# Out product by seven products of quarters, with its sums on GpSimd, in a fused top-k attention and SwiGLU kernel

## The chip, the cores and the metric

The kernel runs on one core of one Trainium2 chip. The metric is the device time of one execution in microseconds (us). The profile names the engines PE (TensorE, matmuls), PEld (its weight loads), DVE (VectorE), ACT (ScalarE), POOL (GpSimd) and SP (SyncE, which issues the transfers). Each engine works through its own instructions in the order in which they were written, and engines wait for each other through semaphores.

## The reference

Attention keeps, in each row of scores, only the 32 largest; the result is laid out as 4608 tokens by 512 and goes through a gated feed-forward layer. All is fp32.

```python
# q, k, v: (8, 8, 576, 64); w_gate, w_val: (512, 1536); w_out: (1536, 512)
scores = scale * np.matmul(q, k.transpose(0, 1, 3, 2))
kth = np.partition(scores, -top_k, axis=-1)[..., -top_k:-top_k + 1]     # top_k = 32
scores = np.where(scores >= kth, scores, -1000000000.0)
attn = np.exp(scores - np.max(scores, axis=-1, keepdims=True))
attn = attn / (np.sum(attn, axis=-1, keepdims=True) + 1e-09)
x = np.matmul(attn, v).transpose(0, 2, 1, 3).reshape(B * S, H * D)
g = x @ w_gate
return g * (1.0 / (1.0 + np.exp(-g))) * (x @ w_val) @ w_out
```

## The kernel before

**Attention** goes in 160 units `n`: for each of 8 batches, four full tiles of 128 queries and a rest of 64, each for four pairs of heads. A unit with a rest has half the work. The loop over `n` (L524) holds, in program order: `normalize` of unit n-2 begins (POOL, L312), `penalize` of n-1 (POOL adds the scores to the mask, 128x1152, L293), `turn` of n-3 (PE transposes the weights, L329, ACT copies them out, L330), `values` of n-4 (PE, L349 and L358, ACT copies to `xT`, L373), `scores` of n+1 (PE, L250), `weigh` of n-1 (ACT exp, L302), the copies of the scores of n+1 (ACT, L255), and then the selection for unit n on DVE (L271, L275, L281). Between the steps of the selection stand the slots for the feed-forward layer, the end of `normalize` (DVE L314, ACT L317), and now and then the preparation of keys and queries (`fetch`, PE L205 and L197).

In this text **A** is the PE part of attention in one unit: transposes, values and scores, one after the other.

**The feed-forward layer** goes in 18 blocks `kb` of 256 tokens. `feed(kb)` is a generator. For each of six pairs of 128 columns of d_ff it makes a gate product and a value product (`product`, L412: 2 x 4 matmuls of 256 columns each, into one PSUM bank of `ps_f`, which has three). ACT takes each product out (L430 to L432, L437) and POOL multiplies (L433, L438), so that `h` stands as 128 columns of d_ff by 256 tokens, which is the form in which PE loads it as weights. The out product (L449) then makes, for each of two groups of 128 tokens, 12 matmuls of 512 columns that add up in one bank, with `h` as weights and `wo` as the moving operand. ACT copies the bank (L460) and SP stores it (L389). The block's `xT` buffer isn't read after the value products.

**Who sets the order.** `pieces(n)` draws up to n pieces from `feed` in slots of 2, 1, 1 and 6 per unit (L564, L572, L575, L578), as long as `credit` is at least 1. A piece is one half of a product or four matmul instructions' worth of the out product (two matmuls); each costs one credit. A full unit gets 4.6, a half unit 2.3, and at most 8 are saved up. A block can only begin when all its tokens have left attention (`done`, L479). What ACT and POOL have to do for a piece is put into `on_act` and `on_pool` and written out by `flush`: at the top of a unit (L545, L549), after the first slot (L565), or when more than one thing is waiting. At the end (L585 to L598) the order of each engine is fixed as it was written.

**Weights** come as 64-bit numbers and are rounded to fp32 in the kernel by `weights` (72 pieces, spread over the first units by `rounding`), with ACT, POOL and DVE at work on each.

Of the kernel before, what the change touches and what calls it, by code (L numbers as in the profile page):

```python
# [9 lines left out]
ALU = mybir.AluOpType  # L10
# [5 lines left out]
P = 128  # L16
# [4 lines left out]
BLK = 256  # L21
# [6 lines left out]
def kernel(  # L28
# [24 lines left out]

    nc = tc.nc
    B, H, S, D = q.shape
    DM, DFF = w_gate.shape
# [4 lines left out]
    KC = DM // P  # L63
    MC = DFF // P
    MS = MC // 2
    NBLK = B * S // BLK
    scale = 1.0 / float(D) ** 0.5
    assert D == 64 and R == 64 and H * D == DM and DM == 512 and B * S % BLK == 0
# [52 lines left out]
    def weights():  # L121
# [11 lines left out]
        for n in range(len(pieces) + lags[0]):  # L133
# [3 lines left out]
            ready[0] = max(n - lags[0] + 1, 0)  # L137
            yield

    ready = [0]  # L140
    weight = weights()

    def rounding(n):
# [254 lines left out]
    def feed(kb):  # L398
# [7 lines left out]
        def product(w, s, then):  # L406
            ps = ps_f.tile([P, 2, BLK], FP32, tag="f", name="f")
            need(8 * s + (4 if w is wg else 8))
            for i in range(2):
                m = 2 * s + i  # L410
                for kc in range(KC):
                    nc.tensor.matmul(  # L412
                        ps[:, i, :],
                        w[:, kc, m * P : (m + 1) * P],
                        x[:, kc, :],
                        start=(kc == 0),
                        stop=(kc == KC - 1),
                    )
                if i == 1:
                    on_act.append(lambda: then(ps))  # L420
                yield

        for s in range(MS):
            h = ffn.tile([P, 2, BLK], FP32, tag="h", name="h", bufs=MS + 1)
# [7 lines left out]
                nc.scalar.add(h[:], h[:], 1.0)  # L432
                on_pool.append(lambda: nc.gpsimd.tensor_mul(h[:], h[:], half[:]))  # L433

            def value(ps, h=h):
                val = ffn.tile([P, 2, BLK], FP32, tag="gv", name="val", bufs=3)
                nc.scalar.copy(val[:], ps[:])  # L437
                on_pool.append(lambda: nc.gpsimd.tensor_mul(h[:], h[:], val[:]))  # L438

            yield from product(wg, s, gate)  # L440
            yield from product(wv, s, value)
        for t in range(BLK // P):
            ps = ps_f.tile([P, DM], FP32, tag="f", name="o_ps")
            for m in range(MC):
                need(8 * MS + 2 * m + 2)
                if m == 6:
                    flush(on_act)
                    flush(on_pool)
                nc.tensor.matmul(  # L449
                    ps[:],  # L450
                    hs[m // 2][:, m % 2, t * P : (t + 1) * P],
                    wo[:, m, :],
                    start=(m == 0),
                    stop=(m == MC - 1),
                )
                if m == MC - 1:

                    def finish(ps=ps, t=t):
                        o = ffn.tile([P, DM], FP32, tag="o", name="o")
                        nc.scalar.copy(o[:], ps[:])  # L460
                        store(o, kb * BLK + t * P)

                    on_act.append(finish)
                if m % 2 == 1:
                    yield

    NU = len(units)
    todo = list(range(NBLK))
# [2 lines left out]
    def piece():  # L471

        if len(on_act) > 1:
            flush(on_act)
        if len(on_pool) > 1:
            flush(on_pool)
        while True:
            if not current:
                if not todo or done.get(todo[0], 0) < NHP * BLK:  # L479
                    return False  # L480
                flush(on_act)
                flush(on_pool)
                current.append(feed(todo.pop(0)))
            if next(current[0], 0) == 0:
                current.pop()
                continue
            return True

    def fetch(n):

# [6 lines left out]

    def pieces(n):
        for _ in range(n):
            if credit[0] >= 1 and piece():  # L500
                credit[0] -= 1

    def run(steps):
        for _ in steps:
# [19 lines left out]
    for n in range(NU + VALUES):  # L524
# [16 lines left out]
        if n >= NU - NHP:  # L541
            credit[0] = 8.0
        else:
            credit[0] = min(credit[0] + (4.6 if nh == 2 else 2.3), 8.0)
        flush(on_act)  # L545
        next(norm, None)
        if 0 <= n - 1 < NU:
# [81 lines left out]
```

## Time and profile before

| | us |
|---|---|
| median of 6 runs (lowest, highest) | 1914.99 (1913.37, 1916.08) |
| profiled execution, its own time | 1916.66 |
| its span from first to last instruction | 1914.9 |
| PE busy in the span | 1757.5 |
| DVE busy | 1609.0 |
| ACT busy | 1156.3 |
| POOL busy | 813.4 |

The span is the time from the first instruction to the last; the execution's own time has 1.8 us more around it. Busy times of PE are modelled, since matmuls overlap each other; a group's mean of one matmul is therefore longer than the distance from one to the next, and the pace of a run of matmuls is read from the starts in the timeline. One fp32 matmul of the program stands as two instructions in the profile. Before about 280 us the weights arrive and the pipeline fills; from there to about 1795 us the kernel is in a steady state; after 1847 us only the last block is left.

### The profile page before, as it was taken

What the parts mean: (1) busy time and instruction counts of PE and PEld (TensorE: products, weight loads), DVE (VectorE), ACT (ScalarE), POOL (GpSimd) and SP (SyncE); (2) the same over time, 40 slices, a digit from 0 to 9 for tenths busy, and PEclk for the clock granted to TensorE, in tenths of its full rate; (3) what the DMA queues carried; (4) which work ended last, traced back from release to release, by engine and by line L of the source; (5) the groups of instructions that cost most, each with busy time, mean ns of one, the idle gap of its engine ahead of it and who ended that gap; (6) DMA issues with size and microseconds to landing.
All of it is one profiled execution on the core that took longest, in us unless ns stands there. A gap on an engine that the chain in (4) does not pass through costs nothing.

```text
span 1914.9 us, 29363 instructions
## 1 busy us (share of the span) xinstructions
PE 1757.5 (92%) x10144; PEld 1298.7 (68%) x10144; DVE 1609.0 (84%) x3476; ACT 1156.3 (60%) x2821; POOL 813.4 (42%) x846
## 2 busy tenths in 40 slices
PE   3437789979999999999899999999999999999999
PEld 2326558667677777676768676868686868586866
DVE  7999889998899979998799979999799989999400
ACT  5656656566666656675657566656675656665421
POOL 4566644335343525353335343525243535253412
PEclk7577899989999999999999999999999999999999
DMA  7322202000300012000210003000210001000000
GB/s 184 88 78 83 67 22 68 11 1 2 72 17 12 2 27 62 12 1 13 53 37 1 12 3 87 1 12 1 58 32 12 1 14 45 18 1 12 1 12 11
DMA packets 111254, 59.58 MB, mean 31 GB/s; under 512 B 89089, under 2 KB 97281, under 8 KB 111105
## 3 DMA queue, kind: packets, MB, share of 16 engines
q1 hardware_dynamic: 109904, 57.41, 11.4%
q8 instruction: 80, 1.31, 0.3%
q14 instruction: 70, 0.57, 0.1%
q10 hardware_dynamic: 1200, 0.30, 0.1%
HBM read 48.23 MB, written 9.44 MB: 30 GB/s over the span
## 4 chain that ended last, share of the span: by engine, by line
PE 80%; DVE 7%; POOL 5%; ACT 4%; issue 3%; DMA 0%; SPq 0%; POOLq 0%; DVEq 0%; ACTq 0%
PE f L412 38%; PE o_ps L449 18%; PE av L358 7%; PE etps L329 7%; PE s L250 6%; DVE m L271 3%; DVE rest L275 3%; POOL e L293 2%; PE s L236 2%; PE av L349 1%; ACT e L302 1%; PE kqps L205 1%; ACT sc L255 1%; POOL size L113 1%; POOL size L103 1%
## 5 line engine op out<-in xcount | busy, mean ns | idle before, releaser
L271 DVE MAX8 m<-rest 128x8 f32<-128x576 f32 x864 | 615.3, 747 | 2.2
L275 DVE MATCH_REPLACE8 rest<-m,rest 128x576 f32<-128x576 f32 x576 | 424.2, 743 | 0.0
L412 PE MATMUL f<-xT,wg 128*128 128x256 f32 x1728 | 407.7, 386 | 0.0
L293 POOL TENSOR_TENSOR e<-e,sc 128x1152 f32<-128x1152 f32 (+1 forms) x160 | 382.5, 2390 | 43.6 <-DVE e L281 35.5
L412 PE MATMUL f<-xT,wv 128*128 128x256 f32 x1728 | 396.5, 381 | 0.0
L449 PE MATMUL o_ps<-wo,h 128*128 128x512 f32 x864 | 387.6, 598 | 0.0
L412 PEld LDWEIGHTS f<-xT,wg 128*128 128x128 f32 x1728 | 324.1, 191 | 71.5 <-issue 30.0
L412 PEld LDWEIGHTS f<-xT,wv 128*128 128x128 f32 x1728 | 326.0, 190 | 53.7 <-issue 10.6
L433 POOL TENSOR_TENSOR h<-h,half_g 128x512 f32<-128x512 f32 x108 | 138.2, 1279 | 453.7 <-ACT h L432 438.7
L271 DVE MAX8 m<-sc 128x8 f32<-128x576 f32 x288 | 205.7, 751 | 125.5 <-ACT sc L255 79.3
L329 PE MATMUL etps<-ident,e 128*128 128x128 f32 (+1 forms) x1312 | 188.2, 289 | 127.7 <-POOL size L103 46.9
L449 PEld LDWEIGHTS o_ps<-wo,h 128*128 128x128 f32 x864 | 159.4, 190 | 193.3 <-issue 186.5
L329 PEld LDWEIGHTS etps<-ident,e 128*128 128x128 f32 (+1 forms) x1312 | 160.2, 148 | 177.3 <-issue 54.2
L330 ACT COPY et<-etps 128x512 f32<-128x512 f32 (+1 forms) x448 | 184.7, 482 | 149.3 <-PE etps L329 148.0
L302 ACT ACTIVATE e<-e,bias 128x576 f32<-128x576 f32 x288 | 222.1, 776 | 76.6 <-POOL e L293 76.2
L317 ACT ACTIVATE e<-e,tot 128x576 f32<-128x576 f32 x288 | 210.4, 780 | 5.4 <-DVE tot L314 5.1
L275 DVE MATCH_REPLACE8 rest<-m,sc 128x576 f32<-128x576 f32 x288 | 211.9, 742 | 0.0
L438 POOL TENSOR_TENSOR h<-h,val 128x512 f32<-128x512 f32 x108 | 139.2, 1289 | 149.9 <-ACT val L437 149.9
L250 PE MATMUL s<-kqT 64*128 64x288 f32 x1024 | 173.9, 448 | 9.3 <-ACT kqT L210 5.7
L312 POOL TENSOR_SCALAR tot<-tot 128x2 f32<-128x2 f32 (+1 forms) x160 | 36.4, 227 | 330.7 <-ACT e L302 322.3
L358 PE MATMUL av<-et,v 128*64 128x128 f32 (+1 forms) x2560 | 172.6, 280 | 0.0
L255 ACT COPY sc<-s 128x288 f32<-128x288 f32 x512 | 165.1, 410 | 3.3 <-PE s L250 3.3
(44 smaller groups left out, 1436.1 us busy)
## 6 DMA issues: line engine op xcount, KB each, us to landing
kq_in<-in_k_dram SPq DMA_DIRECT2D x64, 128.0 KB, 2.9
v<-in_v_dram SPq DMA_DIRECT2D x32, 256.0 KB, 3.0
kq_in<-in_q_dram SPq DMA_DIRECT2D x62, 128.0 KB, 3.1
w<-in_moe_w_gate_dram SPq DMA_DIRECT2D x24, 256.0 KB, 2.8
w<-in_moe_w_val_dram SPq DMA_DIRECT2D x24, 256.0 KB, 2.7
w<-in_moe_w_out_dram SPq DMA_DIRECT2D x24, 256.0 KB, 2.6
out_dram<-o SPq DMA_DIRECT2D x40, 128.0 KB, 2.4
out_dram<-o SPq DMA_DIRECT2D x16, 256.0 KB, 2.3
```

What stands on the lines that cost most here:

```text
L250: nc.tensor.matmul(ps[:, 0:half], slab[d, q0 : q0 + P], slab[d, k0 : k0 + half])
L255: nc.scalar.copy(sc[:, i * half : (i + 1) * half], ps[:, 0:half])
L271: nc.vector.max(m[:, t, 8 * r : 8 * r + 8], cur[:, hs])
L275: nc.vector.match_replace(rest[:, hs], m[:, t, 8 * r : 8 * r + 8], cur[:, hs], LOWEST)
L293: nc.gpsimd.tensor_tensor(e[:, every], e[:, every], sc[:, every], ALU.add)
L302: nc.scalar.activation(e[:, hs], e[:, hs], AF.Exp, bias=bias[:, t : t + 1], scale=scale, accum_out=tot[:, t : t + 1],)
L317: nc.scalar.mul(e[:, hs], e[:, hs], tot[:, t : t + 1])
L329: nc.tensor.transpose(ps[0:kl, c * P : (c + 1) * P], e[:, k0 : k0 + kl], ident[:])
L330: nc.scalar.copy(et[0:kl, c0 : c0 + cn, :], ps[0:kl, 0 : cn * P].rearrange("p (c j) -> p c j", c=cn),)
L358: nc.tensor.matmul(av[hh * R : (hh + 1) * R, 0:ql], v_last[:, hh, :] if c == J else vt[:, hh, c, :], moving, start=last and c == 0, stop=c ...
L412: nc.tensor.matmul(ps[:, i, :], w[:, kc, m * P : (m + 1) * P], x[:, kc, :], start=(kc == 0), stop=(kc == KC - 1),)
L449: nc.tensor.matmul(ps[:], hs[m // 2][:, m % 2, t * P : (t + 1) * P], wo[:, m, :], start=(m == 0), stop=(m == MC - 1),)
```

## The change

Blocks 1 to 17 make the out product by Strassen's algorithm in Winograd's form. Rows are the two groups of 128 tokens (`early`, `late`), the inner dimension is cut into two halves of 768, and the output into two halves of 256 columns (`lo`, `hi`). Seven products of quarters take the place of eight: each is six matmuls of 256 columns. Their operands and the output are put together from sums:

- Of the weights, once: `t3`, `t1` (written over `wo`), `t2` and `t4` are differences of quarters of `wo`, made on POOL in `weights()` after the rounding; `t1` and those that follow wait until block 0, which still does the plain out product, has issued its last matmul. They lie in the buffers of the rounding, which is over by then.
- Of `h`, in each block: four sets of three POOL instructions of 128x256, one set before each of the products 1, 7, 5 and 4. In the order of the products: `s32 = early - late` (read by product 7), `late = late + late of the other half` (product 5), `s32 = late - early` (product 6), `late = early of the other half - s32` (product 3). `s32` lies in the block's `xT` buffer. The order of the products is 1, 7, 5, 6, 4, 3, 2.
- Of the products: ACT copies them out in four instructions (`keep_x`, `keep_y`, `rest_x`, `rest_y`), and six POOL instructions (`tt`) add them up: four of 128x256 and two of 128x512. Three of these, in `sum_up`, follow `keep_y`; they are written to POOL's queue ahead of the fourth set of differences, which product 3 reads.

One `o` tile of 128x2x512 takes the place of two of 128x512, and both halves of a block are stored at its end. A piece of a quarter product is three matmuls and costs 0.75 credits; a full unit gets 4.45 and a half unit 2.25.

```diff
@@ -53,6 +53,16 @@
 
 
 
     nc = tc.nc
     B, H, S, D = q.shape
     DM, DFF = w_gate.shape
@@ -63,6 +73,7 @@
     KC = DM // P
     MC = DFF // P
     MS = MC // 2
+    MQ = MC // 2
     NBLK = B * S // BLK
     scale = 1.0 / float(D) ** 0.5
     assert D == 64 and R == 64 and H * D == DM and DM == 512 and B * S % BLK == 0
@@ -137,7 +148,41 @@
             ready[0] = max(n - lags[0] + 1, 0)
             yield
 
+        add, sub = ALU.add, ALU.subtract
+        lo, hi = slice(0, DM // 2), slice(DM // 2, DM)
+        for m in range(0, MQ, 2):
+            mm, nn = slice(m, m + 2), slice(MQ + m, MQ + m + 2)
+            t3 = ffn.tile([P, 2, DM // 2], FP32, tag="w", name="t3", bufs=6)
+            nc.gpsimd.tensor_tensor(t3[:], wo[:, nn, hi], wo[:, mm, hi], sub)
+            T[7] += [t3[:, i, :] for i in range(2)]
+            yield
+        while not plain_done:
+            yield
+        for m in range(0, MQ, 2):
+            mm, nn = slice(m, m + 2), slice(MQ + m, MQ + m + 2)
+            t1 = wo[:, mm, hi]
+            nc.gpsimd.tensor_tensor(t1, t1, wo[:, mm, lo], sub)
+            T[5] += [wo[:, m + i, hi] for i in range(2)]
+            yield
+            t2 = ffn.tile([P, 2, DM // 2], FP32, tag="w", name="t2", bufs=6)
+            nc.gpsimd.tensor_tensor(t2[:], wo[:, nn, hi], t1, sub)
+            T[6] += [t2[:, i, :] for i in range(2)]
+            yield
+            for i in range(2):
+                tag, bufs = ("size", 4) if m + i < 4 else ("ulps", 2)
+                t4 = conv.tile([P, DM // 2], FP32, tag=tag, name="t4", bufs=bufs)
+                nc.gpsimd.tensor_tensor(t4[:], wo[:, MQ + m + i, lo], t2[:, i, :], sub)
+                T[4].append(t4[:])
+            yield
+        T[1] += [wo[:, m, lo] for m in range(MQ)]
+        T[2] += [wo[:, MQ + m, lo] for m in range(MQ)]
+        T[3] += [wo[:, MQ + m, hi] for m in range(MQ)]
+        yield
     ready = [0]
+    plain_done = []
+    T = {i: [] for i in range(1, 8)}
     weight = weights()
 
     def rounding(n):
@@ -418,7 +463,14 @@
                     )
                 if i == 1:
                     on_act.append(lambda: then(ps))
-                yield
+                yield 1
+        plain = kb == 0
+        early, late = slice(0, P), slice(P, BLK)
+        s32 = x[:].rearrange("p a b -> p (a b)")[:, 0 : MQ * P].rearrange(
+            "p (m t) -> p m t", t=P
+        )
 
         for s in range(MS):
             h = ffn.tile([P, 2, BLK], FP32, tag="h", name="h", bufs=MS + 1)
@@ -432,37 +484,142 @@
                 nc.scalar.add(h[:], h[:], 1.0)
                 on_pool.append(lambda: nc.gpsimd.tensor_mul(h[:], h[:], half[:]))
 
-            def value(ps, h=h):
+            def value(ps, h=h, s=s):
                 val = ffn.tile([P, 2, BLK], FP32, tag="gv", name="val", bufs=3)
                 nc.scalar.copy(val[:], ps[:])
                 on_pool.append(lambda: nc.gpsimd.tensor_mul(h[:], h[:], val[:]))
 
             yield from product(wg, s, gate)
             yield from product(wv, s, value)
-        for t in range(BLK // P):
-            ps = ps_f.tile([P, DM], FP32, tag="f", name="o_ps")
-            for m in range(MC):
-                need(8 * MS + 2 * m + 2)
-                if m == 6:
-                    flush(on_act)
-                    flush(on_pool)
+        o = ffn.tile([P, 2, DM], FP32, tag="o", name="o", bufs=1)
+        if plain:
+            for t in range(2):
+                ps = ps_f.tile([P, DM], FP32, tag="f", name="o_ps")
+                for m in range(MC):
+                    need(8 * MS + 2 * m + 2)
+                    if m == 6:
+                        flush(on_act)
+                        flush(on_pool)
+                    nc.tensor.matmul(
+                        ps[:],
+                        hs[m // 2][:, m % 2, t * P : (t + 1) * P],
+                        wo[:, m, :],
+                        start=(m == 0),
+                        stop=(m == MC - 1),
+                    )
+                    if m == MC - 1:
+                        def finish(ps=ps, t=t):
+                            nc.scalar.copy(o[:, t, :], ps[:])
+                            store(o[:, t, :], kb * BLK + t * P)
+                        on_act.append(finish)
+                        if t == 1:
+                            plain_done.append(True)
+                    if m % 2 == 1:
+                        yield 1
+            return
+        while len(T[3]) < MQ:
+            next(weight)
+        DH = DM // 2
+        y_ps = ps_f.tile([P, 2, DH], FP32, tag="f", name="y_ps")
+        x_ps = ps_f.tile([P, 2, DH], FP32, tag="f", name="x_ps")
+        def tt(out, in0, in1):
+            nc.gpsimd.tensor_tensor(out, in0, in1, ALU.add)
+        def quarter(i, ps):
+            for m in range(MQ):
+                s, r = m // 2, m % 2
+                lhsT = {
+                    1: lambda: hs[s][:, r, early],
+                    2: lambda: hs[s + MS // 2][:, r, early],
+                    3: lambda: hs[s][:, r, late],
+                    4: lambda: hs[s + MS // 2][:, r, late],
+                    5: lambda: hs[s][:, r, late],
+                    6: lambda: s32[:, m],
+                    7: lambda: s32[:, m],
+                }[i]()
                 nc.tensor.matmul(
-                    ps[:],
-                    hs[m // 2][:, m % 2, t * P : (t + 1) * P],
-                    wo[:, m, :],
-                    start=(m == 0),
-                    stop=(m == MC - 1),
+                    ps, lhsT, T[i][m], start=m == 0, stop=m == MQ - 1
                 )
-                if m == MC - 1:
-
-                    def finish(ps=ps, t=t):
-                        o = ffn.tile([P, DM], FP32, tag="o", name="o")
-                        nc.scalar.copy(o[:], ps[:])
-                        store(o, kb * BLK + t * P)
-
-                    on_act.append(finish)
-                if m % 2 == 1:
-                    yield
+                if m % 3 == 2:
+                    yield 0.75
+        for s in range(MS // 2):
+            nc.gpsimd.tensor_tensor(
+                s32[:, 2 * s : 2 * s + 2], hs[s][:, :, early], hs[s][:, :, late], ALU.subtract
+            )
+        yield from quarter(1, y_ps[:, 0])
+        flush(on_act)
+        flush(on_pool)
+        for s in range(MS // 2):
+            nc.gpsimd.tensor_tensor(
+                hs[s][:, :, late], hs[s][:, :, late], hs[s + MS // 2][:, :, late], ALU.add
+            )
+        yield from quarter(7, x_ps[:, 1])
+        for s in range(MS // 2):
+            nc.gpsimd.tensor_tensor(
+                s32[:, 2 * s : 2 * s + 2], hs[s][:, :, late], hs[s][:, :, early], ALU.subtract
+            )
+        yield from quarter(5, x_ps[:, 0])
+        a = ffn.tile([P, 2, DH], FP32, tag="gv", name="p57", bufs=3)
+        def keep_x():
+            nc.scalar.copy(a[:], x_ps[:])
+            on_pool.append(lambda: tt(o[:, 1, DH:], a[:, 0], a[:, 1]))
+        on_act.append(keep_x)
+        b = ffn.tile([P, 2, DH], FP32, tag="gv", name="p16", bufs=3)
+        def keep_y():
+            nc.scalar.copy(b[:], y_ps[:])
+            def sum_up():
+                tt(b[:, 1], b[:, 0], b[:, 1])
+                tt(o[:, 1, DH:], o[:, 1, DH:], b[:, 1])
+                tt(a[:], a[:], b[:, 1:2].to_broadcast([P, 2, DH]))
+            on_pool.append(sum_up)
+        yield from quarter(6, y_ps[:, 1])
+        on_act.append(keep_y)
+        flush(on_act)
+        flush(on_pool)
+        for s in range(MS // 2):
+            nc.gpsimd.tensor_tensor(
+                hs[s][:, :, late],
+                hs[s + MS // 2][:, :, early],
+                s32[:, 2 * s : 2 * s + 2],
+                ALU.subtract,
+            )
+        x_ps2 = ps_f.tile([P, 2, DH], FP32, tag="f", name="x_ps")
+        yield from quarter(4, x_ps2[:, 1])
+        yield from quarter(3, x_ps2[:, 0])
+        middle = o[:].rearrange("p t d -> p (t d)")[:, DH : 3 * DH].rearrange(
+            "p (t d) -> p t d", t=2
+        )
+        def rest_x():
+            nc.scalar.copy(middle, x_ps2[:])
+            on_pool.append(lambda: tt(middle, middle, a[:]))
+        on_act.append(rest_x)
+        y_ps2 = ps_f.tile([P, DH], FP32, tag="f", name="y_ps")
+        yield from quarter(2, y_ps2[:])
+        def rest_y():
+            nc.scalar.copy(o[:, 0, 0:DH], y_ps2[:])
+            def stores():
+                tt(o[:, 0, 0:DH], o[:, 0, 0:DH], b[:, 0])
+                for t in range(2):
+                    store(o[:, t, :], kb * BLK + t * P)
+            on_pool.append(stores)
+        on_act.append(rest_y)
 
     NU = len(units)
     todo = list(range(NBLK))
@@ -477,14 +634,15 @@
         while True:
             if not current:
                 if not todo or done.get(todo[0], 0) < NHP * BLK:
-                    return False
+                    return 0
                 flush(on_act)
                 flush(on_pool)
                 current.append(feed(todo.pop(0)))
-            if next(current[0], 0) == 0:
+            cost = next(current[0], 0)
+            if cost == 0:
                 current.pop()
                 continue
-            return True
+            return cost
 
     def fetch(n):
 
@@ -497,8 +655,8 @@
 
     def pieces(n):
         for _ in range(n):
-            if credit[0] >= 1 and piece():
-                credit[0] -= 1
+            if credit[0] >= 1:
+                credit[0] -= piece()
 
     def run(steps):
         for _ in steps:
@@ -541,7 +699,7 @@
         if n >= NU - NHP:
             credit[0] = 8.0
         else:
-            credit[0] = min(credit[0] + (4.6 if nh == 2 else 2.3), 8.0)
+            credit[0] = min(credit[0] + (4.45 if nh == 2 else 2.25), 8.0)
         flush(on_act)
         next(norm, None)
         if 0 <= n - 1 < NU:
```

## The prediction

> **What bounds the kernel now.** I read the page's first part, then the chain that ended last, then busy time by stretches of 100 us, then the timeline of a unit, then the rows by shape.
>
> ```profile
> PE 1757.5 (92%) x10144; PEld 1298.7 (68%) x10144; DVE 1609.0 (84%) x3476; ACT 1156.3 (60%) x2821; POOL 813.4 (42%) x846
> ...
> PE 80%; DVE 7%; POOL 5%; ACT 4%; issue 3%; DMA 0%; SPq 0%; POOLq 0%; DVEq 0%; ACTq 0%
> ```
>
> ```profile
> 1000.00:1100.00 100.00, 100.00 (x576) 75.51 (x577) 92.34 (x199) 64.88 (x154) 41.84 (x39) 1.00 0.03 6
> 1100.00:1200.00 100.00, 99.33 (x621) 73.06 (x620) 86.90 (x184) 64.61 (x159) 41.18 (x44) 1.00 0.17 43
> ```
>
> The columns of the stretches are us, then busy PE, PEld, DVE, ACT, POOL, clock, DMA share, GB/s. In the steady state PE has no gaps: time taken off PE is time gained, and a new PE wait is lost. DVE is close behind (92%), POOL has 58% free. In the timeline one unit with an out product, PE and ACT:
>
> ```profile
> 1066.93 1.15 PE L329 MATMUL etps<-ident,e 128*128 128x128 f32 x9
> 1067.57 1.24 ACT L330 COPY et<-etps 128x512 f32<-128x512 f32 x3 [1.57 <-PE etps L329]
> 1069.54 0.78 ACT L302 ACTIVATE e<-e,bias 128x576 f32<-128x576 f32 x1
> 1070.43 8.85 PE L449 MATMUL o_ps<-wo,h 128*128 128x512 f32 x20
> 1071.07 1.28 ACT L255 COPY sc<-s 128x288 f32<-128x288 f32 x4
> 1072.22 1.47 ACT L317 ACTIVATE e<-e,tot 128x576 f32<-128x576 f32 x2
> 1079.12 1.15 PE L329 MATMUL etps<-ident,e 128*128 128x128 f32 x9
> ```
>
> Counted from the unit's start, A takes PE 3.5 us (to 1070.43), and ACT is tied up by attention until 5.4 (score copies) and, with L317, until about 6.8. What ACT is to copy in between stands behind that. The rows by shape give POOL's prices:
>
> ```profile
> L293 POOL TENSOR_TENSOR e<-e,sc 128x1152 f32<-128x1152 f32 x128 | 337.3, 2635 | 40.5 <-DVE e L281 32.4 <-PE s L250 4.7 <-PE etps L329 2.4
> L433 POOL TENSOR_TENSOR h<-h,half_g 128x512 f32<-128x512 f32 x108 | 138.2, 1279 | 453.7 <-ACT h L432 438.7 <-DVE rest L275 15.0
> L113 POOL TENSOR_TENSOR size<-size,ulps 128x256 int32<-128x256 int32 x72 | 53.2, 739 | 68.3 <-DVE size L110 54.7 <-ACT et L330 6.3 <-ACT ulps L106 2.4
> ```
>
> **PE's saving.** Weight loads of the out product follow each other at 0.429 us (1905.21 to 1909.50, ten of them): 48 instructions of 512 columns take 20.6 us. Gate and value instructions, which have 256 columns, follow at 0.2156 (16 from 1016.18 to 1019.63): the new 7 x 6 x 2 = 84 take 18.1. Saved: 2.48 a block, 42.1 in 17 blocks. Weight loads (0.19) stay under the matmul (0.2156), as they do in the gate product now.
>
> **POOL's load.** Per block 12 differences and 4 sums of 128x256 at 0.74, two sums of 128x512 at 1.28: 14.4 us, 16.0 with a gap of 0.09 after each (1007.55 + 1.28 to 1008.92); no row shows halves of 128 apart, half of 1279 (0.64) is the lower bound. Over 17 blocks that is 245 us busy, which the free 58% would hold. But it falls into the stretch of about 2.4 units in which a block's products run. There POOL also has L293 with its two small instructions (3.2 a unit) and the last multiplications: about 26 us of work in some 27 us of PE's. And PE and POOL wait for each other by turns.
>
> **Where PE waits.** Three sets have cover: differences before product 7 begin when the last value product ends (2.5 us, behind product 1's 2.6 or more), those before 5 and 6 follow pair by pair. The fourth, before product 3, hangs on a chain that begins when product 6 ends: drain 0.20, ACT's keep_y 0.59, to POOL 0.14, sum_up 0.74 + 0.74 + 1.28 with 0.27 of gaps, one difference 0.74, back to PE 0.1: 4.8 us. Only product 4 lies in between, 12 x 0.2156 = 2.59. The bare wait is 2.2 us. It goes where A falls between 6's end and 3, after 4 has begun; it grows where ACT or POOL comes late. The issue order of the changed program says which. I walked each pattern by the rows above.
>
> - Blocks 5, 10, 14 (6, 4 and 3 in one unit). In the unit before, POOL has 3.2 + 1.37 + 9 x 0.83 = 12 us against PE's 11.3, so its next L293 ends at 3.8, exp runs from 3.85, scores are out at 6.65, keep_x at 7.25, L317 at 8.7, keep_y at 9.3, sum_up at 12.5, the first difference at 13.3. PE is through with 4 at 3.5 + 2.6 + 2.6 = 8.7: 4.65 each.
> - Blocks 4, 13 (half of 5 first). POOL is 5.7 us into the unit when L293 ends; keep_y at 11.2, difference at 15.2 against 10.0: 5.3 each.
> - Blocks 6, 7, 15 (A between 6 and 4). keep_y stands behind A's ACT work, out at 6.05, difference at 10.1 against 6.1: 4.05 each.
> - Blocks 2, 11 (the same in half units): 2.5 each. Block 1: 3.2. Block 9: 2.7. Block 17, alone: 2.2.
> - Blocks 3, 8, 12, 16 have A or most of it inside 4 or before 3: no wait there. But L293 of the next unit is behind POOL's sums, so exp, score copies and L317 come 6 us late, and the transposes after that wait: 1.5 for each of the first three, 0.3 for 16.
>
> Sum: 49.9 in 13 waits, 4.8 for the rest. Bounds: 13 x 2.2 = 29 and no rest, or 13 x 5.3 = 69 and 10 for the rest. I take the walk, since its ACT times are those of a unit in this trace.
>
> **The clock after a wait.** PE stood still for 2.4 to 2.7 us six times between 386 and 1665 and 6 us once.
>
> ```profile
> 402.74 2.15 PE L329 MATMUL etps<-ident,e 128*128 128x128 f32 x9 [5.98 <-issue]
> ...
> 1276.20 2.16 PE L329 MATMUL etps<-ident,e 128*128 128x128 f32 x9 [2.69 <-issue]
> ```
>
> At both, nine transposes take 2.15 instead of 1.15, and at 1276.20 the granted clock has a dip to half for 3.4 us. Of the six, three (912, 1276, 1664) were followed so, at about 1.6 us each; 386, 393 and 792 were not. Half of 13 waits at 1.6 is 10.4; bounds 0 and 13 x 1.6 = 21.
>
> The Trainium skill, page "TensorE: Matmul & The Clock Gate", section "Why this matters for your kernels", asks for no gaps over about 3 us between bursts, since an idle window brings half rate. It speaks against this change; in this trace gaps of 2.4 to 2.7 were already enough half of the time. By the page the nine waits over 3 us would all dip and the others none: 9 x 1.6 = 14.4 instead of 10.4, and the sum 4 us longer.
>
> **The rest.** Differences of weights: 9 x 1.28 + 6 x 0.74 = 16 us of POOL around 250 to 400 us, in front of L293 in its queue, one set waiting for block 0's last matmul. POOL is half idle there and PE at 88 to 91%; I take 2 us, bounds 0 and 8 (half on the path). Tail: the last ACT copy is 256 columns wide (about 0.35 for 0.59), then a POOL sum (0.74 + 0.14): +0.7. Two stores of 128 rows are issued together at the end instead of one; the transfer is bounded by its 2.4, take 0.1, so +0.8. Two more ACT copies a block (of 512 and 256) stand in the walk. Weight pieces, DVE's instructions and SP's loads keep their counts. DVE's selection isn't slowed by a busy POOL: MAX8 and MATCH_REPLACE8 take 0.745 whether POOL works or not. PSUM and the single `o` tile are covered: their readers are done a block earlier.
>
> **Sum.** -42.1 + 49.9 + 4.8 + 10.4 + 2 + 0.8 = +25.8. The profiled execution took 1916.66 (span 1914.9), 1.7 above the median; on the median's footing 1914.99 + 25.8, so 1940.
>
> **Rivals.**
>
> - *The waits stay bare (faster).* Place: product 3's first matmul. Price: at 2.2 each, 13 x 2.2 = 28.6, with the rest 4.8 + 2 + 0.8 and no dips, -42.1 + 36.2 = -5.9: 1909. It decides below a mean wait of 2.66 without dips ((42.1 - 7.6) / 13), or 1.9 with them. For it: ACT is free 40% of the time. Against it: in these units ACT's attention work ends later than product 6 does. Chance 0.15.
> - *Every sum is hidden (faster).* Only the saving: -42.1 + 2.8 gives 1876. Against it: the chain of 4.8 is in the instruction order, its cover is 2.6. Chance 0.03.
> - *Even.* Waits of 2.66 to 3.2 and few dips: 1912 to 1919. Chance 0.07.
> - *POOL becomes the bound of the stretch and its lateness goes round (slower still).* L293 late makes exp, scores, then DVE late, and DVE at 92% recovers little: another 2 us in each block, 1940 + 34 = 1974. For it: 26 us of POOL in 27; against it: the empty units after many blocks (A alone) let POOL catch up. Chance 0.12.
> - *The forecast*, 1922 to 1962: 0.63.
>
> **How the numbers follow.** Lowest by the bounds: -42.1 + 28.6 + 0.8 = -12.7, 1902; highest: -42.1 + 69 + 10 + 21 + 8 + 0.8 = +66.7, 1982. The range 1905 to 1968 leaves out the hidden case, the end of the lowest and a part of the POOL case, about 0.2 in all. The forecast's own range is 1922 to 1962. About 0.2% (3.8 us) is what measurements here can tell from no change. Faster: 0.15 + 0.03 = 0.18; same 0.07; slower 0.63 + 0.12 = 0.75.
>
> **What would show it.** PE's matmuls of quarters start 0.2156 apart; PE's busy time falls by about 40. The waits show PE (or PEld) at the quarter products waiting for POOL, some 50 us in 13 places, the longest in blocks 4, 5, 10, 13 and 14. More dips of the clock than the five after 400 us. POOL busy near 1075. I am wrong if PE's waits for POOL sum to under 35 us, or if keep_y starts right after product 6 in full units.

## The result, and the profile after

| | before | after |
|---|---|---|
| median (lowest to highest), us | 1914.1 (1910.2–1916.67, 32 runs) | 1920.3 (1918.43–1921.45, 14 runs) |
| span of the profiled execution | 1914.9 | 1919.7 |
| PE busy | 1757.5 | 1731.4 |
| granted clock at half, from 270 us to the last matmul | 27.3 us in 5 stretches | 47.8 us in 9 |

The ratio is 1.003, with the interval [1.0023, 1.0037]: slower by 6.2 us. The sign was forecast, the size was not (+25.8). "Half clock" below is the time in which PE's granted clock stood at half.

The page of the changed kernel begins like this (engines with busy time, share and instructions; then the shares of the chain that ended last):

```profile
PE 1731.4 (90%) x10756; PEld 1422.6 (74%) x10756; DVE 1620.5 (84%) x3476; ACT 1169.5 (61%) x2855; POOL 1060.4 (55%) x1167
...
PE 70%; POOL 10%; DVE 9%; ACT 7%; issue 3%; DMA 0%; SPq 0%; POOLq 0%; ACTq 0%; DVEq 0%
```

PE is busy for 26.1 us less, and yet the span is 4.8 longer: PE now stands still for 31 us more. On the chain PE has lost ten points (80% before), half of them to POOL. The same two stretches of 100 us as before (busy PE, PEld, DVE, ACT, POOL, then clock, DMA share, GB/s):

```profile
1000.00:1100.00 100.00, 99.65 (x618) 83.62 (x619) 91.25 (x194) 65.89 (x157) 57.54 (x60) 1.00 0.03 6
1100.00:1200.00 100.00, 97.18 (x655) 79.61 (x654) 88.74 (x188) 64.05 (x159) 54.27 (x60) 1.00 0.17 43
```

POOL went from 41 to 54–58 in both. The first stretch has the out product of block 8, which doesn't wait; the second that of block 9, which does (2.09 us at 1169.68), and there PE is down from 99.33 to 97.18. What PE waits for, in us, times and longest:

```profile
PE x_ps L543 <- POOL h L591: 29.5, 13, 3.2
PE etps L374 <- issue: 27.0, 15, 4.0
PE etps L374 <- ACT e L362: 13.0, 10, 4.0
```

and the last two in the kernel before:

```profile
PE etps L329 <- issue: 28.0, 13, 6.0
PE etps L329 <- ACT e L317: 10.9, 8, 1.7
```

The first line of the changed kernel is new: product 3 waits for the fourth set of differences, 13 times, in exactly the 13 blocks of the forecast and in none of 3, 8, 12 and 16. The two lines on transposes together rose by 1.1. A full unit with product 6, 4 and 3 (block 5), which is the first pattern that the prediction walks; columns are start, length, engine, line, operation, and in brackets the idle time before it; rows that don't bear on the chain are left out:

```profile
757.91 1.15 PE L374 MATMUL etps<-ident,e 128*128 128x128 f32 x9
758.24 2.64 POOL L338 TENSOR_TENSOR e<-e,sc 128x1152 f32<-128x1152 f32 x1
760.91 0.77 ACT L347 ACTIVATE e<-e,bias 128x576 f32<-128x576 f32 x1 [0.23 <-POOL e L338]
761.41 2.86 PE L543 MATMUL y_ps<-t,xT 128*128 128x256 f32 x12
762.44 1.27 ACT L300 COPY sc<-s 128x288 f32<-128x288 f32 x4
763.59 0.61 ACT L570 COPY p<-x_ps 128x512 f32<-128x512 f32 x1
764.07 1.47 ACT L362 ACTIVATE e<-e,tot 128x576 f32<-128x576 f32 x2
764.10 2.75 PE L543 MATMUL x_ps<-t,h 128*128 128x256 f32 x12
765.41 0.60 ACT L577 COPY p<-y_ps 128x512 f32<-128x512 f32 x1
766.09 0.72 POOL L529 TENSOR_TENSOR p<-p 128x256 f32<-128x256 f32 x1 [1.02 <-ACT p L577]
766.89 0.73 POOL L529 TENSOR_TENSOR o<-o,p 128x256 f32<-128x256 f32 x1
767.58 1.27 POOL L529 TENSOR_TENSOR p<-p,p 128x512 f32<-128x512 f32 x1
768.80 2.10 POOL L591 TENSOR_TENSOR h<-h,xT 128x256 f32<-128x256 f32 x3
769.58 4.54 PE L543 MATMUL x_ps<-wo,h 128*128 128x256 f32 x12 [2.73 <-POOL h L591]
```

The whole chain can be followed. Product 6 (761.41) is through at 764.10, where product 4 begins, and `keep_y` (L577) could start. It starts at 765.41, since on ACT the score copies (L300), `keep_x` (L570) and L362 stand before it. `sum_up` takes POOL three instructions (L529), and only then do the differences come (L591). Product 3 starts when the first of them is out, 2.73 us after product 4 gave PE up. Its 12 matmuls then take 4.54 instead of 2.75: the clock is at half.

### The profile page after: what moved, and what is told of

It is laid out like the page before. It is cut to its first block, busy times and chain, and to the rows that moved or that the text cites. A ratio compares the mean times of both kernels' runs of the same rounds, so it can differ in the third digit from the quotient of the medians.

```text
span 1919.7 us, 30988 instructions
## 1 busy us (share of the span) xinstructions
PE 1731.4 (90%) x10756; PEld 1422.6 (74%) x10756; DVE 1620.5 (84%) x3476; ACT 1169.5 (61%) x2855; POOL 1060.4 (55%) x1167
## 4 chain that ended last, share of the span: by engine, by line
PE 70%; POOL 10%; DVE 9%; ACT 7%; issue 3%; DMA 0%; SPq 0%; POOLq 0%; ACTq 0%; DVEq 0%
PE f L457 35%; PE av L403 7%; PE x_ps L543 7%; PE etps L374 7%; PE s L295 5%; PE y_ps L543 4%; DVE m L316 4%; DVE rest L320 4%; POOL e L338 3%; ACT e L347 2%; ACT sc L300 2%; PE s L281 2%; POOL p L529 1%; PE av L394 1%; POOL size L124 1%
## 5 line engine op out<-in xcount | busy, mean ns | idle before, releaser
L338 POOL TENSOR_TENSOR e<-e,sc 128x1152 f32<-128x1152 f32 (+1 forms) x160 | 382.6, 2391 | 26.3 <-DVE e L326 26.0
L374 PE MATMUL etps<-ident,e 128*128 128x128 f32 (+1 forms) x1312 | 190.5, 290 | 128.8 <-POOL size L114 46.3
L362 ACT ACTIVATE e<-e,tot 128x576 f32<-128x576 f32 x288 | 210.7, 782 | 5.4 <-DVE tot L359 5.1
L300 ACT COPY sc<-s 128x288 f32<-128x288 f32 x512 | 164.4, 407 | 3.3 <-PE s L295 3.3
L482 ACT ACTIVATE h<-f 128x512 f32<-128x512 f32 x108 | 64.8, 600 | 165.0 <-PE f L457 164.5
L326 DVE TENSOR_SCALAR e<-sc,m 128x576 f32<-128x576 f32 x288 | 158.8, 588 | 3.8 <-DVE m L316 0.5
L403 PEld LDWEIGHTS av<-et,v 128*64 128x64 f32 x2560 | 137.1, 145 | 23.2 <-issue 7.1
```

Source lines behind the costliest of these rows:

```text
L300: nc.scalar.copy(sc[:, i * half : (i + 1) * half], ps[:, 0:half])
L338: nc.gpsimd.tensor_tensor(e[:, every], e[:, every], sc[:, every], ALU.add)
L362: nc.scalar.mul(e[:, hs], e[:, hs], tot[:, t : t + 1])
L374: nc.tensor.transpose(ps[0:kl, c * P : (c + 1) * P], e[:, k0 : k0 + kl], ident[:])
L403: nc.tensor.matmul(av[hh * R : (hh + 1) * R, 0:ql], v_last[:, hh, :] if c == J else vt[:, hh, c, :], moving, start=last and c == 0, stop=c ...
```

## The experiments

All times are medians; the kernel before, run beside these, had 1912.9 to 1915.7. "Theory A" is the forecast's own: the waits at product 3, with the slow clock behind them, eat the saving. Its rivals are that POOL's load itself costs it, and that the credits do.

**1. The fourth set of differences ahead in POOL's queue.** What it reads is ready long before, and what it writes over was last read by product 5; only its place in the queue puts it behind `sum_up`.

```diff
+        for s in range(MS // 2):
+            nc.gpsimd.tensor_tensor(hs[s][:, :, late], hs[s + MS // 2][:, :, early], ...)
         yield from quarter(6, y_ps[:, 1])
         on_act.append(keep_y)
         flush(on_act)
         flush(on_pool)
-        for s in range(MS // 2):
-            nc.gpsimd.tensor_tensor(hs[s][:, :, late], hs[s + MS // 2][:, :, early], ...)
```

> The fourth set of differences (read by product 3) is written to POOL's queue ahead of product 6 instead of after the sums that follow keep_y, so that products 6 and 4 lie over it. All work is kept. Theory A (the 13 waits before product 3, 29.5 us in the profile, and the half-clock stretches after them decide): PE's waits at the quarter products for POOL fall from 29.5 to under 3 us, the time falls by 30 to 35 us against the changed kernel, to 1885 to 1890 us, 1.3% under the kernel before. Theory B (POOL's load or attention's own chain is the bound, and the waits only show it): PE then waits at the transposes instead, and the time stays at 1905 or more.

Measured: 1880.92 us, ratio 0.9833 [0.9818, 0.9848], 39.4 less than the changed kernel, and more than the 30 to 35 that I expected. No wait of product 3 for POOL is left, and half clock is down by 6.8 us (41.0). POOL's busy time is the same as in the changed kernel:

```profile
PE 1721.3 (92%) x10756; PEld 1418.5 (75%) x10756; DVE 1618.7 (86%) x3476; ACT 1171.3 (62%) x2855; POOL 1062.9 (57%) x1167
```

The saving was there all the time, and the place of three instructions in a queue had used it up. The waits (29.5) and half of the half clock (3.4) are 32.9 of the 39.4. The other 6.5 are not tied to a step; they lie in PE's busy time, which fell by 10.1 and not by 3.4.

**2. The chain longer.** Two more POOL sums, which nobody reads, at the end of `sum_up`.

```diff
                 tt(a[:], a[:], b[:, 1:2].to_broadcast([P, 2, DH]))
+                for _ in range(2):
+                    tt(x[:, 3, :], b[:, 0], b[:, 1])
```

> The changed kernel with two more POOL additions of 128x256 (about 1.4 us) in sum_up, ahead of the fourth set of differences; nobody reads what they write. Theory A: each of the 13 waits before product 3 grows by 1.4 us, 18 us in all, and more half-clock stretches follow, 0 to 10 us: 1938 to 1948 us. Theory B: POOL has 24 us more work of 1060, and the time moves by 1 to 5 us, to 1921 to 1925.

Measured: 1961.79 us, ratio 1.0259 [1.0242, 1.0276], 41.5 more than the changed kernel, far beyond what I expected.

```profile
PE x_ps L543 <- POOL h L593: 50.2, 14, 4.7
```

The waits grew by 20.7, so the length of the chain reaches PE as it should. The other half is the clock: half clock went from 47.8 us to 92.2, and half of the 44.4 more is 22.2. Together 42.9, for 41.5 measured. This counts half clock inside the waits too, where it costs nothing: PE was busy in 43.3 of the 47.8 us and in 79.7 of the 92.2, so the slow clock itself cost 18.2, and the sum is 38.9. The waits at the transposes grew by 1.7.

**3. No differences of `h`.** The kernel leaves out all four sets of differences and multiplies with plain `h`.

```diff
-        for s in range(MS // 2):
-            nc.gpsimd.tensor_tensor(s32[:, 2 * s : 2 * s + 2], hs[s][:, :, early], hs[s][:, :, late], ALU.subtract)
...
-                    6: lambda: s32[:, m],
-                    7: lambda: s32[:, m],
+                    6: lambda: hs[s][:, r, early],
+                    7: lambda: hs[s][:, r, early],
```

> The changed kernel without the four sets of differences of h: products 7, 5, 6 and 3 read plain parts of h, so the output is not the reference's; all seven products, the sums of the products and the copies are kept. Theory A: no wait before product 3, so about the same time as with the early differences, 1880 to 1888 us: POOL's 9 us of differences a block cost nothing but the wait. Theory B: POOL is relieved by 150 us and the time falls well under that with the early differences, below 1875.

Measured: 1877.53 us, ratio 0.9818 [0.9803, 0.9832]; the span is 40.0 below that before. PE's saving, worked out as 42.1, is real: PE stands still for 159.6 us here and for 157.4 before, so it is PE's busy time that fell (1715.3 for 1757.5). The time is 2.5 us under the range of theory A. Against experiment 1, which has all differences and no waits, it gains 3.4 us: that is all the differences cost when PE doesn't wait for them.

**4. POOL's load alone.** The kernel before, with as many POOL instructions per block as the change adds, on a buffer that nobody reads by then.

```diff
+                if kb > 0 and m % 2 == 1:
+                    for _ in range(2 if t == 1 and m < 9 else 1):
+                        nc.gpsimd.tensor_tensor(x[:, 0], x[:, 1], x[:, 2], ALU.add)
+                    if m == 9:
+                        nc.gpsimd.tensor_tensor(x[:, 0:2], x[:, 2:4], x[:, 2:4], ALU.add)
```

> The kernel before with the change's POOL load and nothing else: beside the out product of blocks 1 to 17 POOL makes 16 additions of 128x256 and 2 of 128x512 on the block's xT buffer, which nobody reads any more. Theory A: no one waits for them, the time moves by less than 4 us. Theory B: the load delays attention's additions (L293), exp and the scores, and the kernel gets slower by 15 us or more.

Measured: 1914.9 us, ratio 1.0009 [1.0, 1.0019].

```profile
PE 1757.2 (92%) x10144; PEld 1298.2 (68%) x10144; DVE 1627.1 (85%) x3476; ACT 1155.2 (60%) x2821; POOL 1044.8 (55%) x1152
```

POOL has 231 us more to do and the time moves by at most 4. The rival "POOL becomes the bound" falls, as far as load goes; here nobody waits for the added work, so its place in the queue isn't tested.

**5. Other cover.** Product 2 ahead of product 3, so that two products lie over the chain. Its copy and its sum move with it, and the stores now follow the sum of product 3.

```diff
         yield from quarter(4, x_ps2[:, 1])
+        y_ps2 = ps_f.tile([P, DH], FP32, tag="f", name="y_ps")
+        yield from quarter(2, y_ps2[:])
...
+        on_act.append(rest_y)
         yield from quarter(3, x_ps2[:, 0])
...
-        y_ps2 = ps_f.tile([P, DH], FP32, tag="f", name="y_ps")
-        yield from quarter(2, y_ps2[:])
```

> The changed kernel with product 2 ahead of product 3 on PE; POOL's queue keeps the fourth set of differences behind the sums that follow keep_y. Theory A (what counts is how much PE work lies over the chain from product 6 to product 3): products 4 and 2 cover 5.2 us of a chain of 4.2 to 6, so each wait shrinks by 2.6 and all that remains of 29.5 us is under 3 us; time within 5 us of the version with the early differences, 1878 to 1886. Rival (POOL's order itself was the gain, since attention's L293 came earlier): little of the gain, 1905 or more.

Measured: 1888.38 us, ratio 0.9873 [0.9849, 0.9898], 2 us beyond the range of theory A, and far from the rival's 1905: POOL's queue is as in the changed kernel, so its order as such was not the gain. Three waits of 0.5 to 0.6 us are left at product 3. It stays 7 us behind experiment 1, and PE's waits for L362 at the transposes are 20.6 us (13.0 in the changed kernel, 8.4 in experiment 1), while the other line on transposes falls from 31.3 in experiment 1 to 22.3. Why the first grows I did not follow up.

**6. The chain shorter.** Only the last and longest instruction of `sum_up`, 1.27 us, goes behind the differences.

```diff
                 tt(o[:, 1, DH:], o[:, 1, DH:], b[:, 1])
-                tt(a[:], a[:], b[:, 1:2].to_broadcast([P, 2, DH]))
...
+        tt(a[:], a[:], b[:, 1:2].to_broadcast([P, 2, DH]))
         x_ps2 = ps_f.tile([P, 2, DH], FP32, tag="f", name="x_ps")
```

> The changed kernel with only the last addition of sum_up (128x512, 1.27 us) put behind the fourth set of differences. Theory A with the clock: each wait before product 3 shrinks by about 1.2 us, from 1.3 to 3.2 down to 0.1 to 2.0 us, some 14 us in all; waits this short are not followed by half clock, so the gain is more than 15 us: 1897 to 1903 us. If a wait costs its own length and nothing more: 1904 to 1906.

Measured: 1900.14 us, ratio 0.9929 [0.9915, 0.9944], 20.2 less than the changed kernel.

```profile
PE x_ps L543 <- POOL h L590: 13.6, 11, 2.0
```

The waits are 15.9 us shorter and half clock is down by 10.3 (37.5): 15.9 + 5.1 = 21.0, for 20.2 measured, within the range that I gave. One instruction of 1.27 us in the wrong place cost more than 1% of the kernel.

**7 to 12. The credits.** The change also lowers what a unit may draw from 4.6 (half unit 2.3) to 4.45 (2.25), and the prediction gives no price for that. Six kernels change these two numbers alone, in the kernel before, the changed kernel or the kernel of experiment 1; the diff is in all of them

```diff
-            credit[0] = min(credit[0] + (4.45 if nh == 2 else 2.25), 8.0)
+            credit[0] = min(credit[0] + (4.6 if nh == 2 else 2.3), 8.0)
```

or the same with the numbers of the table. "Early set" is experiment 1.

> The version with the early differences, with the credits of the kernel before (4.6 and 2.3 instead of 4.45 and 2.25): the feed-forward pieces come a little earlier and the blocks wait more often for attention. PE's work is the same; if PE is the bound the time stays within 4 us of 1881, if attention's chain bounds the units the longer units cost 5 us or more.

> The version with the early differences, with credits of 4.3 and 2.2: fewer units without feed-forward work, and so fewer waits of PE for ACT at the transposes (3.7 us each in three places), against more work left at the end, where nothing lies beside it. Within 6 us of 1881; lower if those waits and the half clock after them go, higher if the end grows by more.

> The kernel before with only the credits of the change (4.45 and 2.25). Theory C (the credits are a part of the change with a price of their own: units without feed-forward work, where PE waits 2.7 to 3.7 us for ACT and then runs at half clock, become fewer; 9 in place of 13 here): 8 to 20 us faster than before, 1894 to 1906. Rival (the credits only follow the smaller number of pieces, the plain out product needs 4.6): more is left at the end with nothing beside it, 1912 to 1925.

> The changed kernel with the credits of before (4.6 and 2.3), that is the seven products alone; 18 units without feed-forward work in place of 12. Theory C: slower than the changed kernel by about as much as this step cost the version with the early differences (25 us), 1940 to 1950. Rival (the waits before product 3 let attention catch up, so the empty units cost less here): 1920 to 1930.

> The version with the early differences at credits of 4.2 and 2.15. The units without feed-forward work stay 9, so there is nothing more to win by theory C, and 14 pieces more are left for the end: 1855 to 1870. If the gain from 4.45 to 4.3 came from shorter units rather than from the empty ones, it goes on: below 1850.

> The changed kernel, waits before product 3 and all, at credits of 4.3 and 2.2. If the two effects add up (39 us for the waits at 4.45, 25 for this step of the credits): 1890 to 1900.

| kernel | credits | us | ratio to the kernel before | units without feed-forward work, after 250 us, without the last two of attention | waits at transposes (issue + ACT) |
|---|---|---|---|---|---|
| before | 4.6 / 2.3 | 1914.1 | 1 | 6 | 38.9 |
| before | 4.45 / 2.25 | 1894.05 | 0.9887 [0.9873, 0.9902] | 2 | 25.0 |
| changed | 4.6 / 2.3 | 1954.53 | 1.0205 [1.019, 1.022] | 11 | 62.7 |
| changed | 4.45 / 2.25 | 1920.3 | 1.003 [1.0023, 1.0037] | 5 | 40.0 |
| changed | 4.3 / 2.2 | 1899.35 | 0.9915 [0.9898, 0.9931] | 2 | 25.4 |
| early set | 4.6 / 2.3 | 1906.17 | 0.9961 [0.9947, 0.9975] | 11 | 51.4 |
| early set | 4.45 / 2.25 | 1880.92 | 0.9833 [0.9818, 0.9848] | 5 | 39.7 |
| early set | 4.3 / 2.2 | 1855.77 | 0.9699 [0.9685, 0.9713] | 2 | 23.2 |
| early set | 4.2 / 2.15 | 1847.75 | 0.9648 [0.9634, 0.9662] | 2 | 14.0 |

(The expectations count these units in another way.) I had expected that the early set would stand within some us of 1881 whatever the credits; 25 us either way says no. Experiments 9 and 12 came out inside their ranges, at an end, experiment 10 slower than its range, experiment 11 faster. With 4.6 the early set has two more waits at transposes, 9.2 us, which the trace puts down to POOL and the last column leaves out. Three of the lines behind the last column: the early set with 4.6, with 4.3 and with 4.2.

```profile
PE etps L374 <- issue: 39.9, 14, 5.4
```

```profile
PE etps L374 <- issue: 15.8, 9, 5.9
```

```profile
PE etps L374 <- issue: 10.4, 6, 3.3
```

The arithmetic that the prediction should have done is short. A block's 256 tokens come out of attention in 8 full units (two tiles of 128 queries by four pairs of heads). Its pieces cost 24 + 12 = 36 credits before and 24 + 7 x 2 x 0.75 = 34.5 after. So the pace at which the layer just keeps up is 36 / 8 = 4.5 before and 34.5 / 8 = 4.31 after. Above it (4.6 before, 4.45 and 4.6 after) the layer runs ahead, a block must wait for its tokens, and units come that hold attention only; below it (4.45 before, 4.3 and 4.2 after) only two such units are left, around 400 us, besides one or two among the last of attention. What such a unit does to PE, in the changed kernel:

```profile
1273.85 1.24 PE L295 MATMUL s<-kqT 64*128 64x288 f32 x8
1278.73 2.15 PE L374 MATMUL etps<-ident,e 128*128 128x128 f32 x9 [3.65 <-issue]
1280.68 0.63 PE L394 MATMUL av<-et,vlast 128*128 128x128 f32 x2
1281.24 1.36 PE L403 MATMUL av<-et,v 128*64 128x128 f32 x16
1282.54 1.24 PE L295 MATMUL s<-kqT 64*128 64x288 f32 x8
1283.71 1.56 PE L457 MATMUL f<-xT,wg 128*128 128x256 f32 x6
```

Between the scores at 1273.85 and the next transposes there is nothing for PE; it waits 3.65 us and comes back at half clock (nine transposes in 2.15 instead of 1.15).

So the diff holds two changes of opposite sign. With the credits as they were, the seven products cost 2.05% (1954.53). Going from 4.6 to 4.45 gives the changed kernel 34 us back, and 21.6 us to the plain one (its ratio, 0.9887). With the pace just under the balance in both, the seven products as written still cost 5.3 us (1899.35 against 1894.05), while the early set saves 38.3 (1855.77), or 46.3 at 4.2. The kernel before was not run under 4.45, so what it would still gain there is open. The early set with 4.2 credits is the best of all, 3.5% under the kernel before:

```profile
PE 1710.0 (93%) x10756; PEld 1412.7 (77%) x10756; DVE 1624.5 (88%) x3476; ACT 1169.5 (63%) x2855; POOL 1070.6 (58%) x1167
```

Between 4.3 and 4.2 the number of units in the table is the same and 8 us still go, where I had expected no gain. The traces show most of it at the end of attention, where the table doesn't count: the last transposes but one, and the first product of the last block, with 4.3 and then with 4.2.

```profile
1781.88 1.33 PE L374 MATMUL etps<-ident,e 128*128 128x128 f32 x5 [3.36 <-ACT e L362]
1789.84 5.99 PE L457 MATMUL f<-xT,wg 128*128 128x256 f32 x16
```

```profile
1776.17 0.71 PE L374 MATMUL etps<-ident,e 128*128 128x128 f32 x5
1781.19 3.72 PE L457 MATMUL f<-xT,wg 128*128 128x256 f32 x16
```

With 4.3 the unit before these transposes holds attention only, PE waits 3.36 us, and half clock lasts for 13.7 us. With 4.2 a product of the layer lies there, and the clock stays full. From these transposes to the second product of the block it is 13.79 us against 8.58. With the wait that is 8.6 of the 10.9 us by which the two spans differ.

## Why the prediction was right, and where it was wrong

**PE's saving: right.** Matmuls of quarters start 0.216 us apart, those of the plain out product 0.429: 18.1 against 20.6 a block, 41.7 in 17 blocks for 42.1 predicted. Experiment 3 has 40.0 in the span. It has the new credits as well, but PE's idle time there is that of the kernel before (159.6 against 157.4), so the 40.0 are not theirs.

**Where PE waits: right; how long: wrong. This is the step that failed.** The prediction's sum has 49.9 us in 13 waits (its terms add up to 49.8); there were 29.5. By its own criterion ("under 35 us") it is wrong. The 20.4 us between them are about the whole miss (25.8 − 6.2 = 19.6); the smaller errors below happen to cancel, which is luck.

| blocks | predicted, each | measured |
|---|---|---|
| 4, 13 | 5.3 | 2.01, 2.02 |
| 5, 10, 14 | 4.65 | 2.73, 2.40, 2.73 |
| 6, 7, 15 | 4.05 | 3.17, 3.06, 3.19 |
| 2, 11 | 2.5 | 1.34, 1.33 |
| 1; 9; 17 | 3.2; 2.7; 2.2 | 1.83; 2.09; 1.65 |

The trace shows three errors, all in the walk and all of one sign, in the blocks that I followed row by row; how much of the 20.4 each is worth was not worked out:

- *ACT's and POOL's instructions overlap their neighbours; I added full durations.* In block 5 two L362 of 0.78 end to end take 1.47 together, and `keep_y` starts 1.34 after the pair began; the instruction after `keep_x`, which is 0.61 long, starts 0.48 after it. Three differences on POOL take 2.10 together, where I had 2.49 (0.74 and a gap of 0.09 each). So in block 5 attention's add ended 2.97 us into the unit (walked: 3.8), `keep_y` started at 7.5 (8.7), and product 3 at 11.7 (13.3).
- *The first set doesn't wait for the end of the value products.* The POOL rows of block 4, with the PE row that matters:

```profile
647.89 2.31 POOL L550 TENSOR_TENSOR xT<-h 128x256 f32<-128x256 f32 x3 [2.83 <-PE f L457]
650.17 1.49 POOL L490 TENSOR_TENSOR h<-h,val 128x512 f32<-128x512 f32 x1
651.61 2.10 POOL L558 TENSOR_TENSOR h<-h 128x256 f32<-128x256 f32 x3
653.66 2.10 POOL L563 TENSOR_TENSOR xT<-h 128x256 f32<-128x256 f32 x3
656.33 2.63 POOL L338 TENSOR_TENSOR e<-e,sc 128x1152 f32<-128x1152 f32 x1
```

```profile
648.94 2.75 PE L543 MATMUL y_ps<-wo,h 128*128 128x256 f32 x12
```

  The first set writes into `xT`, and I let it start after the last value product. It began at 647.89, 1.05 us before product 1, when those matmuls were through that read its own part of `xT`. With shorter sets behind it, attention's add (L338) ended 3.5 us after the unit's transposes began (655.41), not 5.7 into the unit, and the wait was 2.01 instead of 5.3.
- *The bare chain is 4.40, not 4.8.* Block 17, alone:

```profile
1904.87 2.75 PE L543 MATMUL x_ps<-t,h 128*128 128x256 f32 x12
1909.27 2.86 PE L543 MATMUL x_ps<-wo,h 128*128 128x256 f32 x12 [1.65 <-POOL h L591]
```

**"keep_y doesn't start right after product 6": right.** In block 5 it is 1.3 us late, behind L362, as said.

**The clock after a wait: right in size, half of it by luck.** Half clock rose by 20.5 us, which is some 10.2 of lost time for 10.4 predicted. But only three of the 13 waits were followed by it, 5.1 of lost time (2.73, 3.06 and 2.40 us, each with 3.4 us of half clock); the rest of the rise is at the transposes: a new stretch of 6.8 us behind a wait of 3.66 at 788, and longer ones where the kernel before had some (1664: 6.8 for 3.4; 1842: 13.7 for 6.8). The Trainium skill ("TensorE: Matmul & The Clock Gate", "Why this matters for your kernels") asks for no gap over about 3 us; here shorter ones were enough where they fell badly. In experiment 2 all ten waits of product 3 of 3.31 us or more were followed by half clock, and in experiment 6 none of them, up to 2.0; between the two, length alone doesn't decide, since 2.40 was followed and 3.17 and 3.19 weren't, and in experiment 12 even 1.87 and 1.90 were.

What decides can be read from the clock's own rows. In each trace half clock begins and ends on a grid of 3.413 us (after 270 us and before the last matmul all edges lie within 0.004 us of it), and where the grid lies differs from run to run. Taking PE's idle time in each interval of the grid, over the 14 traces: half clock began after 113 intervals. All of them had 1.67 us idle or more. Of the 6367 other intervals at full clock only 16 had that much, and none more than 1.96. So the clock fell when PE stood idle for about half of an interval. The wait of 2.40 before 1260.17 lay with 2.23 in one interval. Those of 3.17 and 3.19 were cut in two by the grid, into 1.69 and 1.48, and 1.95 and 1.23. Which of the 13 waits would be followed was not to be had from their lengths.

**The rest.** Transposes +1.1 us (predicted 4.8). The end after the last matmul +0.6 (predicted 0.8). For the differences of the weights PE waits once, 1.6 us at 259.50, where the kernel before waited 3.3 us for POOL; all other waits of PE together came to 113.6 us for 114.0 (predicted 2 more). POOL busy 1060.4 (predicted near 1075). On DVE, MAX8 and MATCH_REPLACE8 kept their 0.74 to 0.75 us, as said, but the third instruction of the selection (L281, now L326) went from 548 to 588 ns on average, and is at 547 in experiment 3, which leaves the differences out.

**The credits: no term of their own.** The sum takes the pattern of the units from the changed program, and has no price for the step from 4.6 to 4.45. Between before and after that came out nearly even, since the cheaper block and the lower pace go together: 6 units without feed-forward work became 5. But it was not seen that the sign of the whole hangs on it. Experiment 10 shows the same seven products at the old pace 39 us slower than before, experiment 12 shows them at 4.3 credits 16 us faster (1899.35 for 1915.7 of the kernel before, run beside it).

**What doesn't add up.** −41.7 + 29.5 + 10.2 + 1.1 + 0.6 − 0.4 = −0.7, and the span rose by 4.8. The waits and the end make up all of PE's 30.9 us of idle time (29.5 + 1.1 + 0.6 − 0.4 = 30.8), so the missing 5.5 us lie in PE's busy time, which fell by 26.1 and not by 31.5. Experiments 1 and 3 put 3.4 us (median) on the differences alone. Whether that is a part of it isn't shown; the rest stays open.

Of the rivals, "the waits stay bare" was the nearest: the mean wait was 2.27, close to its 2.2, and below its limit of 2.66 without dips; with dips its limit was 1.9, and the dips came. "Even" had the time nearly right (1912 to 1919), but for waits of 2.66 to 3.2, which is not what came.

## What to carry to other kernels

Where a fast engine waits for a sum on a slow one, look first at what stands ahead of that sum in the slow engine's queue: here three instructions that nobody needed yet cost 39 us, and moving the needed ones up is a change of a few lines. When the amount of work per block changes, work out again the pace at which it is handed out (work of a block over the units in which its input arrives), since a pace above the balance buys empty units, and a pace just below it (4.2 for 4.31) cost nothing here. When walking a queue by hand, add distances from start to start, read from the timeline, and not the durations of the rows. When pricing the slow clock after a wait, don't go by the wait's length alone.

## What the runs showed that I had not expected

- After 270 us every wait of PE of 3.21 us or more, in all 14 traces, was followed by half clock, and no wait under 1.74 was (of those of 1 us or more); between them it depended on how the wait lay to the clock's grid. The growth of the waits plus half that of the half clock gives 42.9 for 41.5 in experiment 2, and 21.0 for 20.2 in experiment 6.
- 231 us more work on POOL, with PE at 92% and DVE at 84%, moved the time by no more than 0.19% (experiment 4).
- The credits, lowered by 3%, make the kernel before 1.1% faster with not one instruction of the layer changed.
